# First batch: second-step loads all at once into other tiles' buffers, its evictions on two engines, the first MLP group ahead of other groups and weights

## The chip, the cores and the metric

The kernel runs on one core of one Trainium2 chip. The metric is the time on the device in microseconds (us), less is better. The engines that matter are PE (TensorE, matmuls), DVE (VectorE), ACT (ScalarE), POOL (GpSimd) and SP (SyncE, which here only issues DMAs). Each engine works through its own list of instructions in the order written at build time, and waits on semaphores for what other engines or DMAs must have finished first.

## The reference

The input x has 8 batches of 4224 rows of 192 elements, and weight_gen has 8 heads of 7 taps for each row. First a causal convolution whose taps are a softmax of weight_gen, then the Fourier mixing of FNet, a layer norm, and an MLP of 192 to 768 to 192 with ReLU:

```python
w = softmax(weight_gen)                        # over the 7 taps
x = einsum('bshk,bskhg->bshg', w, unfold(x))   # causal, 7 rows back
mixed = real(fft(fft(x, axis=1), axis=2))
u = x + mixed
un = (u - mean(u)) / sqrt(var(u) + 1e-6)       # over the 192 elements
out = u + maximum(un @ w_ch1, 0) @ w_ch2
```

## The kernel before

The 4224 rows of a batch are laid out as 128 partitions times 33, and are worked in 9 groups of 4 (the last has 1). A batch passes through these stages:

- conv: softmax of the taps (maximum and subtraction on DVE, lines 279 and 280, the exponential on ACT, line 282, then sum and reciprocal on DVE, lines 284 to 286), and the weighted sums u on DVE, POOL and PE. The first step of the Fourier transform follows for each group: matmul pg (line 471), two copies of ACT, and two DVE operations (lines 480 and 482) write a tile gt, which SP stores to a scratch tensor g_d in DRAM.
- transform: the second step. Its input is read back from g_d into six tiles g2 (line 507; the last with a second small load, line 509). Each tile has two halves e = 0 and 1: a group of matmuls into a PSUM bank pp (line 517), and evictions of pp into pq (lines 521 to 531): the rows in order, the mirrored rows (for e = 1 with a minus sign), and for the first two tiles a repeated part. That is 14 evictions for each half. There are two banks for pp, shared with eo.
- mix: for each group matmuls eo on pq (line 546), a copy ot of one half by ACT (line 551), and four DVE operations that add the result to u.
- norm: layer norm. For the first three groups of the first batch ("quick", groups 0 to 2) the statistics come from DVE (lines 580 and 581), for the others from ACT. ACT takes the root rs (line 582), DVE the reciprocal (line 593) and minus the mean times it (L596), and ACT writes un in four parts (line 601). For the quick groups un lies in two PSUM banks that are named like those of the MLP ("ph", three in number, taken in turn). Then un is split into two halves of 16 bits, hl: a cast on ACT (line 609) and two subtractions on DVE (lines 610 and 612; on POOL for later groups). A DMA transposes hl into ht (line 618).
- mlp: for each group six chunks ph (line 643), each five matmuls on ht and the halves of the first weight matrix, in a bank "ph"; ACT evicts each with ReLU to hh (line 649, or 653 with DVE's 654). The second matmuls po (line 666) run one group behind, and the result is added to u and stored.

The weights arrive as 64-bit numbers in words and are rebuilt by seven DVE operations for each piece (words_to_f32, lines 204 to 215). prep_w1 does this for the first matrix, with an ACT cast (line 220) and a DVE subtraction (line 221) for the halves w1h and w1l; eight copies by DMA (line 247) put the last rows in place. prep_w2 does it for the second matrix in three parts, w2_0, w2_1 and w2_2. Before the second step PE runs matmuls on values nobody needs (warm_pp, 20 of them; in the profile each shows as two records), and again before the first MLP group (warm_hl).

What sets the order. The stages are generators. The code adds them to a list of streams with a start and an end on a scale of groups (add), and run() draws them in turn; that is the order of priority. The build's scheduler then lays out each engine's list by this order and by its own simulated times. tc.issue_after(ins) keeps what stands inside from being laid out before ins; behind(ins, gen) does the same for each step of a generator, and queue(ins, ...) for a function. So the lists printed below are what the build made of it, and neither SP's nor any other engine's list changes at run time.

## Time and profile before

| | |
|---|---|
| median of 3 runs | 1138.15 us (1135.78 to 1138.86) |
| profiled execution: span from first to last instruction, the only time of it that the page gives | 1136.8 us |
| PE busy | 1082.2 us, 95% |
| DVE busy | 968.2 us, 85% |
| ACT busy | 814.5 us, 72% |
| POOL busy | 866.7 us, 76% |
| second step of batch 0 on PE (pp) | 82.28 to 95.60 us |
| first MLP chunk ph_0_0_0 begins | 115.05 us |
| second chunk ph_0_0_1 begins | 117.95 us |

In the rows of the timeline a time from the start stands first, then the duration of the whole row, the engine, the line, the operation, what it writes and reads, and how many instructions the row holds (x8). In square brackets stands how long the engine was idle before it and what ended that. In rows of stretches each engine's busy time comes with its number of instructions; the granted TensorE clock is 1.00 at full rate and 0.50 at half. In rows of waits the sum, the number and the longest are given.

### The profile page before, as it was taken

Reading aid. Unit: us, or ns where it says so; the run is one execution under the profiler, and the core shown is the slowest. Engines: PE = TensorE matmul, PEld = TensorE weight load, DVE = VectorE, ACT = ScalarE, POOL = GpSimd, SP = SyncE. Lnnn points to the kernel's source line nnn. Section 1 sums busy time; section 2 is a strip of 40 time slices with the busy share of each in tenths; the row PEclk is TensorE's granted clock in tenths of the full one; section 3 lists DMA queues with packets and bytes.
Section 4 is the critical chain, followed back from the end, with each engine's and each line's share of the span. In section 5 each row is a group of like instructions: output and inputs, shape, how many; then the busy total and the mean of one; then the engine's idle time right before and its main releaser. Section 6 shows DMA issues by size and latency. Waiting matters only on the chain.

```text
span 1136.8 us, 23769 instructions
## 1 busy us (share of the span) xinstructions
PE 1082.2 (95%) x8476; PEld 819.3 (72%) x8476; DVE 968.2 (85%) x1797; ACT 814.5 (72%) x2556; POOL 866.7 (76%) x747
## 2 busy tenths in 40 slices
PE   5986999999999999899999999999999999999998
PEld 3454677787777767677767877777768877787777
DVE  7988999879989999899988999999989996356443
ACT  4666785468975798568974799568965898589822
POOL 5979588699979999599969999699959999012200
PEclk9996999999999999999999999999999999999999
DMA  8353244614473248414562348414661234413221
GB/s 304 129 150 106 56 110 123 175 51 128 111 200 92 65 119 219 122 55 119 149 165 81 94 107 218 121 44 119 170 140 50 71 74 98 115 43 74 70 47 46
DMA packets 156504, 128.74 MB, mean 113 GB/s; under 512 B 108571, under 2 KB 133088, under 8 KB 156384
## 3 DMA queue, kind: packets, MB, share of 16 engines
q1 hardware_dynamic: 156384, 127.21, 42.2%
q8 instruction: 67, 1.10, 0.4%
q14 instruction: 53, 0.43, 0.1%
HBM read 61.46 MB, written 39.37 MB: 89 GB/s over the span
## 4 chain that ended last, share of the span: by engine, by line
PE 52%; DVE 16%; ACT 11%; issue 8%; POOL 7%; DMA 6%; SPq 1%; DVEq 0%; POOLq 0%; ACTq 0%
PE ph L643 22%; PE po L666 19%; DVE pr L441 6%; POOL u L450 6%; PE pp L517 4%; PE eo L546 3%; DMA g<-g_d 2%; ACT junk L590 2%; ACT junk L586 2%; PE pg L471 2%; PE pa L446 2%; ACT hh L653 2%; ACT un L601 2%; DVE hh L654 2%; DMA g_d<-gt 1%
## 5 line engine op out<-in xcount | busy, mean ns | idle before, releaser
L450 POOL TENSOR_TENSOR u<-u,pr 128x768 f32<-128x768 f32 (+1 forms) x390 | 644.5, 1675 | 71.0 <-DVE pr L441 49.6
L666 PEld LDWEIGHTS <-hh 128*128 128x128 f16 x4248 | 364.0, 98 | 74.1 <-DVE hh L654 2.2
L666 PE MATMUL po<-w2h,hh 128*128 128x192 f16 x2832 | 413.9, 246 | 1.2 <-DVE hh L654 1.0
L643 PE MATMUL ph<-ht,w1h 128*128 128x512 f16 (+1 forms) x1296 | 397.0, 363 | 5.4 <-DMA ht<-hl 2.5
L441 DVE TENSOR_TENSOR pr<-x_sb,wp 128x768 f32<-128x768 f32 (+1 forms) x415 | 354.5, 877 | 13.7 <-POOL u L450 9.9
L666 PE MATMUL po<-w2l,hh 128*128 128x192 f16 x1416 | 345.2, 246 | 0.0
L654 DVE SCALAR_TENSOR_TENSOR hh<-ph,hh 128x512 f16<-128x512 f32 (+1 forms) x390 | 246.4, 637 | 108.0 <-ACT hh L653 107.4
L653 ACT ACTIVATE hh<-ph 128x512 f16<-128x512 f32 (+1 forms) x390 | 213.3, 550 | 140.8 <-PE ph L643 114.6
L643 PE MATMUL ph<-ht,w1l 128*128 128x512 f16 (+1 forms) x864 | 311.2, 363 | 0.0
L643 PEld LDWEIGHTS <-w1h 128*128 128x128 f16 x1296 | 126.1, 99 | 93.2 <-issue 2.3
L601 ACT ACTIVATE un<-u,rs 128x192 f32<-128x192 f32 x264 | 123.7, 536 | 16.7 <-POOL hl L612 5.5
L643 PEld LDWEIGHTS <-w1l 128*128 128x128 f16 x864 | 85.4, 99 | 52.9 <-issue 5.3
L590 ACT ACTIVATE junk<-u,rs 128x192 f16<-128x192 f32 x252 | 114.2, 454 | 3.6
L610 POOL TENSOR_TENSOR hl<-un,hl 128x512 f16<-128x512 f32 (+1 forms) x69 | 75.2, 1090 | 51.9 <-issue 26.5
L586 ACT ACTIVATE junk<-u 128x192 f16<-128x192 f32 x252 | 90.8, 360 | 21.5 <-DVE u L556 17.9
L521 ACT COPY pq<-pp 97x204 f32<-97x204 f32 (+1 forms) x96 | 46.9, 489 | 57.4 <-PE pp L517 57.0
L546 PE MATMUL eo<-cs_sb,pq 97*128 97x97 f32 x544 | 84.2, 277 | 2.7 <-DVE u L556 2.7
L546 PEld LDWEIGHTS eo<-cs_sb,pq 97*128 97x128 f32 x544 | 78.1, 195 | 10.2 <-issue 4.7
L671 DVE SCALAR_TENSOR_TENSOR u<-po,isc,u 128x384 f32<-128x384 f32 (+1 forms) x122 | 72.8, 597 | 9.1 <-PE po L666 9.0
L464 POOL TENSOR_TENSOR sm<-u 128x382 f32<-128x382 f32 x64 | 65.3, 1021 | 5.8 <-DMA g_d<-gt 2.8
L599 POOL TENSOR_TENSOR rs<-rs 128x4 f32<-128x4 f32 (+1 forms) x63 | 12.8, 206 | 70.7 <-DVE rs L593 70.6
L666 PE MATMUL po<-w2f,hh 128*128 128x192 f32 x336 | 62.6, 328 | 0.0
(110 smaller groups left out, 1319.5 us busy)
## 6 DMA issues: line engine op xcount, KB each, us to landing
out_dram<-u SPq DMA_DIRECT2D x64, 384.0 KB
x_sb<-in_x_dram SPq DMA_DIRECT2D x48, 384.0 KB
g<-g_d SPq DMA_DIRECT2D x40, 336.0 KB
x_sb<-in_x_dram SPq DMA_DIRECT2D x8, 864.0 KB
g_d<-gt SPq DMA_DIRECT2D x32, 195.0 KB
g_d<-gt SPq DMA_DIRECT2D x32, 189.0 KB
w<-in_weight_gen_dram SPq DMA_DIRECT2D x6, 924.0 KB
x_sb<-in_x_dram SPq DMA_DIRECT2D x8, 672.0 KB
```

The lines of the kernel that those rows point to most:

```text
L441: last_product[b] = nc.vector.tensor_tensor(out=dst, in0=rows, in1=wk, op=ALU.mult)
L450: adder.tensor_tensor(out=u, in0=u, in1=pr, op=ALU.add)
L546: nc.tensor.matmul(eo[:, e, j, :], lhsT=pq[0:DH, e, r, r:r + P], rhs=cs_sb[:, e, :], start=True, stop=True)
L586: nc.scalar.activation(junk, uv[:, t, :], AF.Identity, accum_out=st[:, t, 0:1])
L590: nc.scalar.activation(junk, uv[:, t, :], AF.Square, bias=rs[:, 2, t:t + 1], accum_out=st[:, t, 1:2])
L601: nc.scalar.activation(halves[t // 2][:, t % 2, :], uv[:, t, :], AF.Identity, bias=rs[:, 1, t:t + 1], scale=rs[:, 0, t:t + 1])
L610: lo_eng.tensor_tensor(out=hl[:, t0:t1, 2 * P:3 * P], in0=src[:, 0:t1 - t0, 0:P], in1=hl[:, t0:t1, 0:P], op=ALU.subtract)
L643: last_ph[n] = nc.tensor.matmul(ph[:, 0:T], lhsT=wt[:, cs_], rhs=ht[:, 0:T, blk], start=(i == 0), stop=(i == len(terms) - 1))
L653: nc.scalar.activation(a[:, 0:T], ph[:, 0:T], AF.Relu)
L654: nc.vector.scalar_tensor_tensor(out=l[:, 0:T], in0=ph[:, 0:T], scalar=0.0, in1=a[:, 0:T], op0=ALU.max, op1=ALU.subtract)
L666: nc.tensor.matmul(po[t // 2][:, t % 2, :], lhsT=hx[:, t], rhs=wx[:, c2, :], start=(c2 == 0 and i == 0), stop=(c2 == NH - 1 and i == len(t ...
L671: nc.vector.scalar_tensor_tensor(out=lt, in0=po[t // 2][:, 0:t % 2 + 1], scalar=scales[0][:, 1:2] if f32 else isc, in1=lt, op0=ALU.mult, o ...
```

## The change

For the first batch alone:

- The six g2 tiles no longer take turns in three buffers. Three have the buffers of g2, two those of gt, and the last one of "fold" (a tile of conv). All their loads can be issued one after the other. The eight copies of w1h and w1l are kept behind the last g2 load.
- Of the evictions of pp the half e = 1 goes to DVE, 14 instructions; e = 0 stays on ACT.
- warm_pp has 32 matmuls, and reads f1_sb, a constant, so that it no longer waits for the last gt.
- A root of a constant is taken on ACT behind the last "up" copy of conv, which loads ACT's table for roots there.
- Group 0's un is written by DVE, in four operations that subtract the mean and multiply by rs; L596 falls away for this group.
- Group 2's mix is kept behind the root of group 0, and prep_w2 for parts 0 and 1 is queued after group 0's norm, no longer before its mix.

```diff
@@ -41,7 +41,8 @@
 F32_GROUPS = 7
 ACT_TAPS = {(0, 1): (0,), (0, 3): (0,), (0, 5): (0,1), (0, 7): (0,)}
 TURNS = {1: 'ddpdddd', 2: 'dpddpdd', 3: 'dpddpdp'}
-WARM = (20, 0, 12, 12)
+WARM = (32, 0, 12, 12)
+G2_FIRST = [("g2", TRI, 3)] * 3 + [("gt", TRI, 2)] * 2 + [("fold", 2, 3)]
 
 
 def row_table():
@@ -242,8 +243,8 @@
         w = words_to_f32(raws[0], None, "w1_1", ("ph", 3))
         split_f32(w, hi, lo, s1)
         for src, dst in ((hi, w1h1), (lo, w1l1)):
-            for i in range(2):
-                for j in range(2):
+            for i, j in ((0, 0), (0, 1), (1, 0), (1, 1)):
+                with tc.issue_after(last_g2[0].ins):
                     nc.sync.dma_start(dst[64 * j:64 * j + 64, i * PW:(i + 1) * PW], src[64 * i:64 * i + 64])
         for i in range(2):
             cs_ = slice(i * PW, (i + 1) * PW)
@@ -475,7 +476,7 @@
                 go = gt[:, at:at + J, :]
                 nc.scalar.copy(go[:, :, 0:DH:DH - 1], pg[:, 0:J, 0:DH:DH - 1])
                 up = sb.tile([P, 2, D - DH], F32, tag="up", name=f"up_{b}_{c}", bufs=2)
-                nc.scalar.copy(up[:, 0:J], pg[:, 0:J, DH:D])
+                last_up[b] = nc.scalar.copy(up[:, 0:J], pg[:, 0:J, DH:D])
                 fwd, rev = pg[:, 0:J, 1:DH - 1], up[:, 0:J, ::-1]
                 nc.vector.tensor_tensor(out=go[:, :, 1:DH - 1], in0=fwd, in1=rev, op=ALU.add)
                 last_tile[b] = gt
@@ -502,7 +503,8 @@
         for m0 in range(0, NM, TRI):
             nm = min(TRI, NM - m0)
             full = min(nm, NK1 // 3 - m0)
-            g2 = sb.tile([WL, TRI, D], F32, tag="g2", name=f"g2_{b}_{m0}", bufs=3)
+            home, rows, bufs = G2_FIRST[m0 // TRI] if b == 0 else ("g2", TRI, 3)
+            g2 = sb.tile([WL, rows, D], F32, tag=home, name=f"g2_{b}_{m0}", bufs=bufs)
             first = gv[m0 * W:m0 * W + 1, :]
             last_g2[b] = nc.sync.dma_start(g2[:, 0:full], bass.AP(first.tensor, first.offset, [[D, WL], [W * D, full], [1, D]]))
             if full < nm:
@@ -518,20 +520,24 @@
                                                   rhs=tab[0:kr, 0:w, :], start=True, stop=True)
                     yield (2 * m0 + e * nm + i + 1) / (2 * NM)
                 rows = pq[0:DH, e].rearrange("d r k -> d k r")
-                nc.scalar.copy(rows[:, k0:k0 + nk, :], pp[0:DH, 0:nk, 0:NT])
+                on_dve = b == 0 and e == 1
+                copy = nc.vector.tensor_copy if on_dve else nc.scalar.copy
+                copy(rows[:, k0:k0 + nk, :], pp[0:DH, 0:nk, 0:NT])
                 i0 = 1 if k0 == 0 else 0
                 i1 = nk - 1 if k0 + nk == NK1 else nk
                 dst, src = rows[:, P - k0 - i0:P - k0 - i1:-1, :], pp[0:DH, i0:i1, N2:NT - 1:-1]
                 if e == 0:
                     nc.scalar.copy(dst, src)
+                elif on_dve:
+                    nc.vector.tensor_scalar(out=dst, in0=src, scalar1=-1.0, scalar2=None, op0=ALU.mult)
                 else:
                     nc.scalar.mul(dst, src, -1.0)
                 n = min(KW - P - k0, nk)
                 if n > 0:
-                    nc.scalar.copy(rows[:, P + k0:P + k0 + n, :], pp[0:DH, 0:n, 0:NT])
+                    copy(rows[:, P + k0:P + k0 + n, :], pp[0:DH, 0:n, 0:NT])
 
     state, us, hls = {}, {}, {}
-    last_tile, last_pg, last_product, last_fold, last_gt, last_g2, last_pp = {}, {}, {}, {}, {}, {}, {}
+    last_tile, last_pg, last_product, last_fold, last_gt, last_up, last_g2, last_pp = {}, {}, {}, {}, {}, {}, {}, {}
     pending = {}
     total = B * NG
 
@@ -579,7 +585,7 @@
             for t in range(T):
                 nc.vector.bn_stats(out=bn[:, t, :], in_=uv[:, t, :])
                 last_bn[b, g] = nc.vector.bn_aggr(out=st[:, t, :], in_=bn[:, t, :])
-            nc.scalar.activation(rs[:, 0, 0:T], st[:, 0:T, 1], AF.Sqrt, bias=eps_t)
+            last_sqrt[b, g] = nc.scalar.activation(rs[:, 0, 0:T], st[:, 0:T, 1], AF.Sqrt, bias=eps_t)
             neg = -1.0
         else:
             for t in range(T):
@@ -591,13 +597,20 @@
                                      accum_out=st[:, t, 1:2])
             nc.scalar.activation(rs[:, 0, 0:T], st[:, 0:T, 1], AF.Sqrt, bias=eps_t, scale=1.0 / D)
         nc.vector.reciprocal(out=rs[:, 0, 0:T], in_=rs[:, 0, 0:T])
-        if quick or b == 0:
+        first = NG * b + g == 0
+        if first:
+            pass
+        elif quick or b == 0:
             for t in range(T):
                 nc.vector.tensor_scalar(out=rs[:, 1, t:t + 1], in0=st[:, t, 0:1], scalar1=rs[:, 0, t:t + 1],
                                         scalar2=neg, op0=ALU.mult, op1=ALU.mult)
         else:
             nc.gpsimd.tensor_tensor(out=rs[:, 1, 0:T], in0=rs[:, 2, 0:T], in1=rs[:, 0, 0:T], op=ALU.mult)
         for t in range(T):
+            if first:
+                nc.vector.tensor_scalar(out=halves[t // 2][:, t % 2, :], in0=uv[:, t, :], scalar1=st[:, t, 0:1],
+                                        scalar2=rs[:, 0, t:t + 1], op0=ALU.subtract, op1=ALU.mult)
+                continue
             nc.scalar.activation(halves[t // 2][:, t % 2, :], uv[:, t, :], AF.Identity,
                                  bias=rs[:, 1, t:t + 1], scale=rs[:, 0, t:t + 1])
         yield 0.5
@@ -706,7 +719,7 @@
     def next_conv(b):
         yield from behind(last_product[b - 1].ins, conv(b))
 
-    last_word, last_split, last_lo, last_bn, last_ph, scales = [], [], {}, {}, {}, []
+    last_word, last_split, last_lo, last_bn, last_sqrt, last_ph, scales = [], [], {}, {}, {}, {}, []
     add(0.0, 1.0, conv(0))
     run(0.5)
     loaded = load_weights()
@@ -716,8 +729,11 @@
             for f, arg in calls:
                 f(arg)
 
+    root = cpool.tile([P, 1], F32, name="root")
+    with tc.issue_after(last_up[0].ins):
+        nc.scalar.activation(root, eps_t, AF.Sqrt)
     with tc.issue_after(last_pg[0].ins):
-        WARM[0] and keep_warm(("po", 2), "pp", ident32, last_tile[0][:, 3, 0:P], WARM[0])
+        WARM[0] and keep_warm(("po", 2), "pp", ident32, f1_sb[:, 0], WARM[0])
     add(0.0, 1.0, transform(0))
     run()
     lp = last_product[0].ins
@@ -727,13 +743,16 @@
             break
     tap8, tap9 = ((lambda n: tap_step(1, n), n) for n in (8, 9))
     queue(lp, (prep_w1, loaded[0]))
-    for i in range(2):
-        queue(last_split[-1].ins, (prep_w2, i))
+    split1 = last_split[-1].ins
     for g in range(QUICK):
-        add(0.0, 1.0, behind(last_split[-1].ins, mix(0, g)))
+        gen = behind(split1, mix(0, g))
+        add(0.0, 1.0, behind(last_sqrt[0, 0].ins, gen) if g == 2 else gen)
         run()
         add(0.0, 1.0, norm(0, g))
         run()
+        if g == 0:
+            for i in range(2):
+                queue(split1, (prep_w2, i))
     for g, call in ((0, tap8), (1, (prep_w2, 2)), (1, tap9)):
         queue(last_lo[g].ins, call)
 
```

Line numbers of the changed kernel are 1 to 13 higher than those before: L280 there is L279 here, L588 is L582, L614 is L601, L622 and L623 are L609 and L610, L662 is L649.

On SP, in the second step of batch 0, stood before:

```order
44 L507 DMA g2_0_0_714<-g_d0_89 112x4x192
45 L507 DMA g2_0_4_732<-g_d0_89 112x4x192
46 L507 DMA g2_0_8_750<-g_d0_89 112x4x192
47 L247 DMA w1h1_83<-w1h_1_892 64x384 x4
48 L247 DMA w1l1_84<-w1l_1_893 64x384 x4
49 L507 DMA g2_0_12_766<-g_d0_89 112x4x192
50 L507 DMA g2_0_16_782<-g_d0_89 112x4x192
51 L507 DMA g2_0_20_798<-g_d0_89 112x192
52 L509 DMA g2_0_20_798<-g_d0_89 68x192
```

and now stands:

```order
44 L509 DMA g2_0_0_728<-g_d0_89 112x4x192
45 L509 DMA g2_0_4_746<-g_d0_89 112x4x192
46 L509 DMA g2_0_8_764<-g_d0_89 112x4x192
47 L509 DMA g2_0_12_780<-g_d0_89 112x4x192
48 L509 DMA g2_0_16_796<-g_d0_89 112x4x192
49 L509 DMA g2_0_20_812<-g_d0_89 112x192
50 L511 DMA g2_0_20_812<-g_d0_89 68x192
51 L248 DMA w1h1_83<-w1h_1_906 64x384 x4
52 L248 DMA w1l1_84<-w1l_1_907 64x384 x4
```

The three later tiles' loads moved ahead of the eight copies.

On ACT, from the casts of group 1 (hl_0_1) to the eviction of the first MLP chunk (hh_0_0_0); w_1 is the taps of batch 1, whose exponential L282 this is. Before:

```order
97 L609 CAST hl_0_1_1050<-un_0_1_0_1029 128x2x192
98 L609 CAST hl_0_1_1050<-un_0_1_1_1030 128x2x192
99 L282 ACT_TABLE_LOAD
100 L282 ACTIVATE w_1_812<-w_1_812 128x1344
101 L601 ACTIVATE un_0_2_0_1073<-u_0_2_220,rs_0_2_1071 128x192
102 L601 ACTIVATE un_0_2_1_1074<-u_0_2_220,rs_0_2_1071 128x192
103 L601 ACTIVATE un_0_2_0_1073<-u_0_2_220,rs_0_2_1071 128x192
104 L601 ACTIVATE un_0_2_1_1074<-u_0_2_220,rs_0_2_1071 128x192
105 L609 CAST hl_0_2_1094<-un_0_2_0_1073 128x2x192
106 L649 ACTIVATE hh_0_0_0_1126<-ph_0_0_0_1120 128x512
107 L609 CAST hl_0_2_1094<-un_0_2_1_1074 128x2x192
108 L649 ACTIVATE hh_0_0_1_1137<-ph_0_0_1_1128 128x512
```

and now:

```order
80 L622 CAST hl_0_1_1060<-un_0_1_1_1040 128x2x192
81 L283 ACT_TABLE_LOAD
82 L283 ACTIVATE w_1_826<-w_1_826 128x1344
83 L588 ACT_TABLE_LOAD
84 L588 ACTIVATE rs_0_2_1081<-st_0_2_1080,eps_t_79 128x4
85 L614 ACTIVATE un_0_2_0_1083<-u_0_2_220,rs_0_2_1081 128x192
86 L614 ACTIVATE un_0_2_1_1084<-u_0_2_220,rs_0_2_1081 128x192
87 L614 ACTIVATE un_0_2_0_1083<-u_0_2_220,rs_0_2_1081 128x192
88 L614 ACTIVATE un_0_2_1_1084<-u_0_2_220,rs_0_2_1081 128x192
89 L622 CAST hl_0_2_1104<-un_0_2_0_1083 128x2x192
90 L622 CAST hl_0_2_1104<-un_0_2_1_1084 128x2x192
91 L662 ACTIVATE hh_0_0_0_1136<-ph_0_0_0_1130 128x512
```

The root rs_0_2, which stood eight rows ahead of the exponential before (row 92, behind the casts of hl_0_0), now stands behind the exponential with a table load of its own, and the eviction hh_0_0_0 moved behind both casts of hl_0_2. un_0_2_0 and un_0_2_1 lie in banks "ph", of which ph_0_0_1 takes the first.

On DVE, the last rows ahead of the subtraction L280 (now L281), whose result the exponential takes. Before:

```order
178 L593 RECIPROCAL rs_0_1_1027<-rs_0_1_1027 128x4
179 L580 BN_STATS bn_0_2_1075<-u_0_2_220 128x6 x4
180 L596 TENSOR_SCALAR rs_0_1_1027<-st_0_1_1026,rs_0_1_1027 128x1 x4
181 L581 BN_AGGR st_0_2_1070<-bn_0_2_1075 128x2 x4
182 L610 TENSOR_TENSOR hl_0_0_993<-un_0_0_0_972,hl_0_0_993 128x2x128
183 L612 TENSOR_TENSOR hl_0_0_993<-un_0_0_0_972,hl_0_0_993 128x2x64
184 L610 TENSOR_TENSOR hl_0_0_993<-un_0_0_1_973,hl_0_0_993 128x2x128
185 L612 TENSOR_TENSOR hl_0_0_993<-un_0_0_1_973,hl_0_0_993 128x2x64
186 L279 TENSOR_REDUCE wp_1_811<-w_1_812 128x192
187 L593 RECIPROCAL rs_0_2_1071<-rs_0_2_1071 128x4
188 L280 TENSOR_TENSOR w_1_812<-w_1_812,wp_1_811 128x1344
189 L596 TENSOR_SCALAR rs_0_2_1071<-st_0_2_1070,rs_0_2_1071 128x1 x4
```

and now:

```order
194 L561 TENSOR_TENSOR u_0_2_220<-u_0_2_220,eo_0_2_1069 128x4x97
195 L562 TENSOR_TENSOR u_0_2_220<-u_0_2_220,eo_0_2_1069 128x4x95
196 L605 TENSOR_SCALAR rs_0_1_1037<-st_0_1_1036,rs_0_1_1037 128x1 x4
197 L214 SCALAR_TENSOR_TENSOR t_w2_1_1017<-raw_w4_418,pa_w2_1_1015 128x384
198 L623 TENSOR_TENSOR hl_0_0_983<-un_0_0_0_966,hl_0_0_983 128x2x128
199 L625 TENSOR_TENSOR hl_0_0_983<-un_0_0_0_966,hl_0_0_983 128x2x64
200 L623 TENSOR_TENSOR hl_0_0_983<-un_0_0_1_967,hl_0_0_983 128x2x128
201 L625 TENSOR_TENSOR hl_0_0_983<-un_0_0_1_967,hl_0_0_983 128x2x64
202 L280 TENSOR_REDUCE wp_1_825<-w_1_826 128x192
203 L586 BN_STATS bn_0_2_1085<-u_0_2_220 128x6 x4
204 L216 TENSOR_TENSOR w2f_87<-pw_w2_1_1016,t_w2_1_1017 128x384
205 L281 TENSOR_TENSOR w_1_826<-w_1_826,wp_1_825 128x1344
```

The statistics and the reciprocal of group 2 now stand behind the last hl of group 0 or behind L281, and operations on w2_1 stand where there were none. Between the first L552 (now L558) and this subtraction stand five operations on w2_0 and w2_1 before, ten now.

## The prediction

> **What bounds the kernel now.** I read the page first, then busy time by stretches with the clock granted, then PE's row of the waits, and last the timelines of PE, DVE, ACT and SP between 72 and 130 us.
>
> ```profile
> span 1136.8 us, 23769 instructions
> PE 1082.2 (95%) x8476; PEld 819.3 (72%) x8476; DVE 968.2 (85%) x1797; ACT 814.5 (72%) x2556; POOL 866.7 (76%) x747
> 97.00:120.00 23.00, 10.24 (x40) 5.99 (x39) 22.61 (x76) 13.75 (x28) 22.84 (x16) 0.58 0.27 50
> 120.00:150.00 30.00, 30.00 (x170) 22.15 (x169) 28.08 (x55) 22.50 (x67) 15.31 (x13) 0.98 0.21 45
> 300.00:1100.00 800.00, 787.19 (x6663) 600.50 (x6662) 683.77 (x1238) 610.17 (x1892) 620.87 (x550) 1.00 0.43 110
> PE pp L517 <- DMA g<-g_d: 10.3, 6, 2.9
> ```
>
> The stretches give start and end, length, then busy us (and instructions) of PE, PEld, DVE, ACT, POOL, the granted clock, the DMA share and GB/s. From 120 us on PE is full (30.00 of 30, later 787 of 800) and works through a fixed list, so a shift of the first MLP group is a shift of the end. In 97 to 120 it is DVE that is full (22.61 of 23): the first group waits there for DVE and ACT. The last row, of PE's waits after 120 us, holds the largest idle time left for a late PE to lose itself in: 10.3 us in six pieces, the longest 2.9.
>
> ```profile
> 74.75 4.70 PE L494 MATMUL warm_pp<-gt,ident 128*128 128x128 f32 x40 [1.22 <-DVE gt L482]
> 82.28 0.91 PE L517 MATMUL pp<-te_sb,g 102*97 102x102 f32 x8 [2.83 <-DMA g<-g_d]
> 84.51 1.68 PE L517 MATMUL pp<-te_sb,g 102*97 102x102 f32 x8 [0.51 <-ACT pq L531]
> 90.09 1.06 PE L517 MATMUL pp<-te_sb,g 102*97 102x102 f32 x8
> 92.11 0.94 PE L517 MATMUL pp<-te_sb,g 102*97 102x102 f32 x8
> 94.01 0.56 PE L517 MATMUL pp<-te_sb,g 102*97 102x102 f32 x4
> 95.04 0.56 PE L517 MATMUL pp<-to_sb,g 102*97 102x102 f32 x4 [0.47 <-ACT pq L528]
> 115.92 0.38 PE L643 MATMUL ph<-ht,w1l 128*128 128x512 f16 x1
> 117.95 0.58 PE L643 MATMUL ph<-ht,w1h 128*128 128x512 f16 x1 [1.65 <-ACT hh L649]
> 76.84:80.25 3.41, 2.62 (x24) 1.00 0.28 78
> 80.25:83.66 3.41, 1.38 (x16) 1.00 1.10 267
> 83.66:87.07 3.41, 2.90 (x18) 0.50 0.58 124
> 117.79:121.20 3.41, 3.25 (x11) 0.50 0.11 21
> 121.20:124.61 3.41, 3.41 (x19) 1.00 0.00 0
> ```
>
> The last five rows are PE alone by stretches; the clock stands behind the busy time. Two PE waits lie on the path: for the first g2 tile (2.83 us), and, behind chunk ph_0_0_0 of the first MLP group, for ACT's hh_0_0_0 (to 117.95).
>
> **The loads, at nothing.**
>
> ```profile
> 78.46 1.39 SPq L507 DMA_DIRECT2D g<-g_d  x3
> 85.54 5.10 SPq L507 DMA_DIRECT2D g<-g_d  x3
> ```
>
> The loads that move were issued from 85.54 on, behind the w1 copies. Still no pp matmul waits for one: among the pp rows only the first has a DMA as releaser. The cover is pp itself, at half clock from 83.66. Issued early they should land before 90, so also a faster pp isn't held. The eight w1 copies go behind them, landing some 7 us later, far ahead of ph at 115. The x loads of batch 1 come about 4.5 us earlier; nothing that PE waits for before 150 us needs them. If pp outran the loads, each of three tiles could cost up to the 1.4 us between issues.
>
> **Warming and the clock, a gain of about 2.1 us.** 32 matmuls make 64 records; at 4.70/40 = 0.1175 us each they last 7.5 us. Without the wait for gt (1.22) they begin at about 73.5 and end at 81, leaving 1.3 us before pp in place of 2.83. The stretch 80.25 to 83.66, busy for 1.38, was followed by half clock; it would now be busy for about 2.2. The stretch before it, busy for 2.62, was followed by full clock. So the bound lies between 1.38 and 2.62; 2.2 is nearer the upper end, and where the stretches fall in a run isn't fixed: I take the clock as kept (6 in 10). Then two tiles that took 90.09 - 84.51 = 5.58 us cold take about 1.9 each as at 92.11 to 94.01, a gain of 1.8, and most of the 0.47 before 95.04 goes: 2.1 in all, so pp ends at 93.5. Bounds: 0 with the clock lost, 2.4 with no wait on evictions.
>
> [...]
>
> **Evictions on DVE, at nothing, up to 0.5.** Fourteen of ACT's evictions go to DVE.
>
> ```profile
> 84.61 0.53 ACT L528 ACTIVATE pq<-pp 97x187 f32<-97x187 f32 x1
> 71.92 0.35 DVE L480 TENSOR_TENSOR gt<-pg,up 128x190 f32<-128x190 f32 x1
> 90.23 0.62 DVE L221 SCALAR_TENSOR_TENSOR w1l<-pw_w,sc_w,w1h 128x384 f16<-128x384 f32 x1 [3.24 <-ACT w1h L220]
> 97.20 0.37 DVE L552 TENSOR_TENSOR eo<-eo,ot 128x194 f32<-128x194 f32 x1 [1.18 <-ACT ot L551]
> ```
>
> The trace has no strided eviction on DVE. Bounds: 0.35 (190 elements read from PSUM there) and 0.53 (the same copy on ACT), so 4.9 to 7.4 us; I take 0.35. DVE idles 3.24 before 90.23 and 1.18 before 97.20, 4.4 that cover most; the rest pushes weight work (w2) behind the first group's start, counted next. PE at full clock is held by neither engine for more than a few tenths, since 92.11 to 94.01 shows a tile at 1.9 with ACT doing both halves. DVE reaches group 0 two evictions and two w2 steps behind pp's end, 93.5 + 0.7 + 0.9 = 95.1: just when ot comes, 1.6 us behind pp's end as before (95.60 to 97.20).
>
> **Group 0 on DVE: 2.4 us longer.**
>
> ```profile
> 97.48 0.55 DVE L207 TENSOR_SCALAR pa_w<-raw_w 128x384 int32<-128x384 int32 x1
> 106.73 0.57 DVE L596 TENSOR_SCALAR rs<-st,rs 128x1 f32<-128x1 f32 x4
> 108.80 0.37 DVE L581 BATCH_NORM_AGGREGATE st<-bn 128x2 f32<-128x6 f32 x4
> 110.11 0.28 DVE L612 TENSOR_TENSOR hl<-un,hl 128x128 f16<-128x128 f32 x1
> 111.89 1.55 DVE L280 TENSOR_TENSOR w<-w,wp 128x1344 f32<-128x1344 f32 x1
> 115.36 1.55 DVE L284 TENSOR_REDUCE wp<-w 128x192 f32<-128x1344 f32 x1
> 119.24 1.36 DVE L286 RECIPROCAL wp<-wp 128x192 f32<-128x192 f32 x1
> 102.65 1.28 ACT L582 ACT_TABLE_LOAD   x1
> 109.47 0.30 ACT L582 ACTIVATE rs<-st,eps_t 128x4 f32<-128x4 f32 x1
> 113.96 1.32 ACT L282 ACTIVATE w<-w 128x1344 f32<-128x1344 f32 x1
> 115.19 1.81 ACT L601 ACTIVATE un<-u,rs 128x192 f32<-128x192 f32 x4
> 116.95 0.46 ACT L609 CAST hl<-un 128x384 f16<-128x384 f32 x1
> ```
>
> Between the first L552 and the subtraction L280 (w_1, batch 1's taps; lines here are those of before) stood 5 steps of w2; by the order there are now 10: 5 x 0.46 = 2.3 (0.46 is start to start, 97.48 to 97.94). The four un on DVE come in at 0.28 each, as L612 (bounds 0.26 to 0.55), 1.1. Out go L596 x4 of group 0 (0.48), the aggregates of group 2 (0.37) and one reciprocal (0.13): 1.0. Net +2.4, so L280 ends at 113.44 - 2.1 + 2.4 = 113.7. Up to the last hl of group 0 the same count gives 4 w2 steps more and group 2's four statistics fewer, +1.1 - 2.1: its transpose goes about 1 us earlier. The table load at 102.65 moves ahead of pp, under PE's and DVE's work; with DVE full behind it (22.61 of 23), that brings no more than this 1 us.
>
> **What ph_0_0_1 now waits for: 3.3 us later.** Before, rs_0_2's root ran at 109.47, ahead of the exponential; un_0_2 followed the exponential at once, and hh_0_0_0 came behind its first cast. Now ACT has, in this order, exponential, table load, rs_0_2's root, un_0_2 x4, both casts, hh_0_0_0. The exponential runs 113.75 to 115.05; the load (1.28) and root (0.30) end at 116.65. DVE meanwhile holds the reduction L284 (1.5, from 115.6 to 117.1), then the reciprocal, one w2 step, L285 and the first L596, 0.13 + 0.46 + 0.27 + 0.1: un_0_2 starts at 118.05 in place of 115.19. It takes 1.8, the casts 0.4 each: 120.65. DVE, with the other L596 (0.35), two w2 steps (0.92) and the reciprocal L286 (1.36) behind that, also gets to hl_0_2 at 120.7 and leaves the bank at 121.25. ph_0_0_1 needs un_0_2's bank, so it starts at about 121.3 and not at 117.95: **+3.3**. Bounds: +2.4 with quick un and evictions, +4.5 with both at their dear ends. That ph_0_0_0 itself comes 1 us earlier is worth nothing then: it ends at 115 and its successor is late.
>
> PE idles for 6 us there, 1.65 before. The clock was half in 117.79 to 121.20, with 3.25 us of work, some 1.6 lost; with stretches placed as before the same amount is lost in the next one, elsewhere up to 1.7 more. I take 0.5.
>
> **Sum:** 3.3 + 0.5 = 3.8 on a span of 1136.8: 1140.6. The profiled span stands 1.35 under the median of the runs, 1138.15, so the time is 1138.15 + 3.8 = **1142.0**.
>
> **Rivals.**
> *Cold* (17%): the warming doesn't hold the clock, pp ends as before, and all of group 0 comes 2.1 us later: 1138.15 + 5.9 = 1144.0, to 1146.5 with dear evictions. For it: the 1.3 us that are still idle, and evictions that alternate with weight work on DVE. Against: 64 records in place of 40.
> *Given back* (20%): the delay is lost in a later idle time of PE, at most the longest wait for g2, 2.9: 1138.15 + 3.8 - 2.9 = 1139.1. For it: x loads 4.5 us earlier; against: pg, ahead of each of these waits, is on PE too and shifts with it.
> *Faster* (15%): DVE sets the pace of the exponential and runs ahead by the whole gain: 2.1 of pp and 1.2 of the table load. Then L280 ends at 110.1, the exponential at 111.5, load and root at 113.1, un_0_2 starts by 114.2, casts end by 116.7: ph_0_0_1 at 116.8, 1.1 earlier, and 1.6 of half clock less: 1138.15 - 2.7 = 1135.5. It decides if L280 ends before about 110.3, which needs the w2 steps not to lie in group 0; the order speaks against it, the full DVE of before makes each step taken out worth its time.
> Early loads bringing nothing is in all four.
>
> **How the numbers follow.** 40% for the sum, 1140 to 1144 by its bounds; the rivals as given; 8% for gains that I can't name. The range reaches to the faster case below and the cold one above: 1134.5 to 1146. A measurement here can tell 0.3% (3.4 us) from no change, so slower begins at 1141.6 and faster at 1134.7: slower is three quarters of the sum's case and all of the cold one, 0.47; faster two thirds of its own case, whose row-by-row gain could as well be 3 to 4, and the unnamed gains, 0.18; the same takes the rest, 0.35.
>
> **What would show it.** Right: PE's second group of ph rows starts at 120 to 122 behind a wait of 5 us or more on DVE hl or ACT hh; ACT shows a table load between the exponential and rs_0_2's root; pp ends by 94 at clock 1.0; no pp but the first waits for a DMA. Wrong: ph_0_0_1 before 118, or half clock in pp, or a busy PE in 300 to 1100 us that has won 2 us or more on its 787 of 800.

## The result: 0.45% slower, and the profile after

| | before | changed |
|---|---|---|
| median of 20 runs | 1137.57 us (1133.34 to 1139.60) | 1141.70 us (1136.31 to 1147.47) |
| ratio to before, 95% interval | | 1.0045 (1.0034 to 1.0057) |
| span of the profiled execution | 1136.8 us | 1140.9 us |

The forecast was 1142.0 us, between 1134.5 and 1146.0, with 0.47 for slower. The time is 0.3 us from it. The path to it is another one, as the traces and runs below show: in the profiled execution the first MLP group came 7 us late and not 3.8, and about 3 us of that were given back later.

The page of the changed kernel, its first two lines:

```profile
span 1140.9 us, 23808 instructions
PE 1083.4 (95%) x8500; PEld 822.2 (72%) x8500; DVE 972.0 (85%) x1811; ACT 812.3 (71%) x2539; POOL 867.6 (76%) x747
```

PE's timeline from the warming matmuls to the second chunk of the first MLP group (changed kernel):

```profile
73.43 7.31 PE L495 MATMUL warm_pp<-f_sb,ident 128*128 128x128 f32 x64
83.61 1.09 PE L519 MATMUL pp<-te_sb,g 102*97 102x102 f32 x8 [2.87 <-DMA g<-g_d]
...
86.00 1.68 PE L519 MATMUL pp<-te_sb,g 102*97 102x102 f32 x8
...
96.26 0.56 PE L519 MATMUL pp<-to_sb,g 102*97 102x102 f32 x4 [0.51 <-ACT pq L530]
96.66 2.26 PE L552 MATMUL eo<-cs_sb,pq 97*128 97x97 f32 x16
...
118.67 0.61 PE L656 MATMUL ph<-ht,w1h 128*128 128x512 f16 x1 [1.66 <-ACT w L283]
...
120.35 0.63 PE L656 MATMUL ph<-ht,w1l 128*128 128x512 f16 x1
124.62 0.58 PE L656 MATMUL ph<-ht,w1h 128*128 128x512 f16 x1 [3.63 <-DVE hl L625]
```

The warming ends at 80.7 as reckoned, but the first g2 tile landed at 83.6 instead of 82.2, so PE was idle for 2.87 us all the same. A tile of pp takes over 1.5 us for each half, as before (the row at 86.00 has 1.68 us for 8 matmuls): the granted clock was 0.50 from 84.20 to 91.03. Group 0's first eo follows at 96.66, where before it stood at 95.44:

```profile
95.44 2.51 PE L546 MATMUL eo<-cs_sb,pq 97*128 97x97 f32 x16
```

ph_0_0_1 starts behind a wait on DVE's hl of group 2, at 124.62 in place of 117.95.

The later landing comes from the store of gt ahead of the load. Both kernels issue the last of it at the same time (75.02 before, 75.08 changed), but SP then waits 2.9 us for it before (first row) and 4.2 in the changed kernel (second):

```profile
SPq L507 <- DMA g_d<-gt: 2.9, 1, 2.9
```

```profile
SPq L509 <- DMA g_d<-gt: 4.2, 1, 4.2
```

Why the store took 1.3 us longer in this execution stays open.

ACT in the same kernel, from the table load for the exponential to hh_0_0_0:

```profile
115.14 1.28 ACT L283 ACT_TABLE_LOAD   x1
117.32 1.32 ACT L283 ACTIVATE w<-w 128x1344 f32<-128x1344 f32 x1 [0.90 <-DVE w L281]
118.66 1.28 ACT L588 ACT_TABLE_LOAD   x1
119.96 0.30 ACT L588 ACTIVATE rs<-st,eps_t 128x4 f32<-128x4 f32 x1
121.56 1.82 ACT L614 ACTIVATE un<-u,rs 128x192 f32<-128x192 f32 x4 [1.31 <-DVE rs L605]
123.33 0.84 ACT L622 CAST hl<-un 128x384 f16<-128x384 f32 x2
124.06 0.59 ACT L662 ACTIVATE hh<-ph 128x512 f32<-128x512 f32 x1
```

This is the chain of the prediction, link for link. DVE's timeline in the changed kernel, from the first evictions to the last hl that ph_0_0_1 waits for:

```profile
86.09 0.50 DVE L525 COPY pq<-pp 97x204 f32<-97x204 f32 x1 [3.88 <-PE pp L519]
86.45 0.47 DVE L532 TENSOR_SCALAR pq<-pp 97x187 f32<-97x187 f32 x1
...
98.42 0.37 DVE L558 TENSOR_TENSOR eo<-eo,ot 128x194 f32<-128x194 f32 x1
...
107.53 0.86 DVE L611 TENSOR_SCALAR un<-u,st,rs 128x192 f32<-128x192 f32 x2
...
115.73 1.56 DVE L281 TENSOR_TENSOR w<-w,wp 128x1344 f32<-128x1344 f32 x1
...
118.97 1.57 DVE L285 TENSOR_REDUCE wp<-w 128x192 f32<-128x1344 f32 x1
...
122.16 1.38 DVE L287 RECIPROCAL wp<-wp 128x192 f32<-128x192 f32 x1
...
124.17 0.30 DVE L625 TENSOR_TENSOR hl<-un,hl 128x128 f16<-128x128 f32 x1
```

A strided eviction on DVE takes 0.36 from start to start (86.09 to 86.45), at the low end of the bounds. From L558 to the end of L281 it is 98.42 to 117.29, 18.9 us, where before L552 to the end of L280 took 16.2: the forecast was 2.4 more, it is 2.6.

Of the changed kernel, PE alone in three stretches that overlap (the second ends at 84.20, where the clock falls), then all engines by stretches, then PE's waits behind 120 us:

```profile
80.20:83.60 3.40, 0.54 (x5) 1.00 0.80 197
80.79:84.20 3.41, 0.59 (x7) 1.00 0.99 237
83.60:87.00 3.40, 3.40 (x22) 0.59 1.12 235
```

```profile
120.00:150.00 30.00, 26.37 (x138) 18.34 (x137) 29.96 (x57) 16.82 (x50) 15.21 (x12) 0.86 0.17 33
300.00:1100.00 800.00, 787.82 (x6681) 602.82 (x6680) 683.88 (x1240) 617.38 (x1910) 619.96 (x551) 1.00 0.43 110
```

```profile
PE pp L519 <- DMA g<-g_d: 10.9, 7, 3.6
PE ph L656 <- DVE hl L625: 3.6, 1, 3.6
```

In the first three rows PE goes on at half clock after 0.59 us of work in the 3.41 up to the fall. The waits for g2 tiles are not smaller than before (10.9 against 10.3 us): the late PE has not lost itself in them.

How late PE is, as the start of the ph matmul with the same number in both traces (counted through the whole run, us):

```
ph matmul    before   changed  later by
     1       115.05    118.67     3.62
     6       117.95    124.62     6.67
    16       122.51    129.52     7.01
   121       176.56    183.55     6.99
   211       229.99    233.26     3.27
   301       282.40    292.50    10.09
   601       422.11    426.92     4.81
  1001       617.55    622.06     4.51
  2160      1131.19   1135.26     4.07
```

Up to 180 us the 7 us stay. Then the difference swings between 3 and 10 and ends at 4.1. Part of that is order alone, since the lists themselves differ: read from the traces, at least 1438 of PE's 8412 matmul records (the warming ones left out) stand elsewhere in the changed kernel, and PE's order is that of before again only from 963 us on, in batch 6 (the batches are 0 to 7). The build lays every list out by simulated times, and here a changed head changed them all. The prediction went by the lists around the first group only. A swing by itself is no proof of it: with only the warming changed, whose lists are those of before from 106 us on, the same difference goes from -1.1 to -4.2 and back to -2.5 us.

### The profile page after: what moved, and what is told of

It reads as the page before. It is cut to its first block, busy times and chain, and to the rows that moved or that the text cites. A ratio compares the mean times of both kernels' runs of the same rounds, so it can differ in the third digit from the quotient of the medians.

```text
span 1140.9 us, 23808 instructions
## 1 busy us (share of the span) xinstructions
PE 1083.4 (95%) x8500; PEld 822.2 (72%) x8500; DVE 972.0 (85%) x1811; ACT 812.3 (71%) x2539; POOL 867.6 (76%) x747
## 4 chain that ended last, share of the span: by engine, by line
PE 52%; DMA 3%; POOL 2%; DVE 1%; issue 1%; ACT 1%; SPq 0%; DVEq 0%; POOLq 0%
PE ph L656 22%; PE po L679 21%; PE pp L519 3%; PE eo L552 3%; PE pg L472 2%; DMA g<-g_d 1%; DMA g_d<-gt 1%; POOL u L451 1%; POOL hl L623 0%; DVE pr L442 0%; DVE hh L667 0%; POOL hl L625 0%; DVE wp L285 0%; ACT un L614 0%; ACT w L283 0%
## 5 line engine op out<-in xcount | busy, mean ns | idle before, releaser
L614 ACT ACTIVATE un<-u,rs 128x192 f32<-128x192 f32 x260 | 121.6, 535 | 20.5 <-DVE rs L605 8.0
L623 POOL TENSOR_TENSOR hl<-un,hl 128x512 f16<-128x512 f32 (+1 forms) x69 | 75.8, 1099 | 56.6 <-issue 26.5
L596 ACT ACTIVATE junk<-u,rs 128x192 f16<-128x192 f32 x252 | 114.3, 454 | 4.1
L552 PE MATMUL eo<-cs_sb,pq 97*128 97x97 f32 x544 | 86.9, 276 | 4.2 <-DVE u L562 4.2
L552 PEld LDWEIGHTS eo<-cs_sb,pq 97*128 97x128 f32 x544 | 79.9, 195 | 10.7 <-issue 4.8
L525 ACT COPY pq<-pp 97x204 f32<-97x204 f32 (+1 forms) x90 | 43.8, 487 | 55.9 <-PE pp L519 55.0
```

Source lines behind the costliest of these rows:

```text
L552: nc.tensor.matmul(eo[:, e, j, :], lhsT=pq[0:DH, e, r, r:r + P], rhs=cs_sb[:, e, :], start=True, stop=True)
L596: nc.scalar.activation(junk, uv[:, t, :], AF.Square, bias=rs[:, 2, t:t + 1], accum_out=st[:, t, 1:2])
L614: nc.scalar.activation(halves[t // 2][:, t % 2, :], uv[:, t, :], AF.Identity, bias=rs[:, 1, t:t + 1], scale=rs[:, 0, t:t + 1])
L623: lo_eng.tensor_tensor(out=hl[:, t0:t1, 2 * P:3 * P], in0=src[:, 0:t1 - t0, 0:P], in1=hl[:, t0:t1, 0:P], op=ALU.subtract)
```

## The experiments

All twelve are kernels of which only the part named is edited. Each ratio is to the kernel before, run on the same chip alongside; it need not be the quotient of two medians (late_old_lists has 1141.87 against 1136.53, a quotient of 1.0047, and a ratio of 1.0030). "Head" below is the delay of the 16th ph matmul in the profiled execution against before, where the first group is done with its waits; "end" is that of the last.

Head and end go by one execution of each kernel. In nearly all runs here the span stands 1.8 us under the run's time, so the profile of before is an execution of about 1138.6 us by estimate, while before's medians alongside were 1135.31 (the first four experiments), 1136.53 (the next four) and 1137.77 (the last four). Counted from those medians each end would be 1 to 3 us larger. And some profiles are of the quickest execution of their kernel (exp_late, w2_late, loads alone) or of the slowest (un_only, late_old_lists).

Some kernels are said below, and in the expectations, to have the lists of before behind the head. In the traces the orders of PE, DVE, ACT and POOL agree with before throughout (loads alone), from 106 us on (warming alone), from 182 (changed_no_un, the change without un on DVE and without the wait) and from 208 (evictions alone, and late_old_lists, with 72 warming matmuls); between the head and there some rows of these three stand elsewhere. Those of the run with 40 warming matmuls agree with the changed kernel's from 116 us on.

**The three theories** were these. A: group 2's root and its table load behind the exponential make ph_0_0_1 late. B: DVE's extra work makes it late. C or L: what happens at 120 us doesn't decide, but the lists behind it that are laid out anew. H stands against L: a shift of the head is a shift of the end.

### Group 2's mix set free

```diff
-        add(0.0, 1.0, behind(last_sqrt[0, 0].ins, gen) if g == 2 else gen)
+        add(0.0, 1.0, gen)
```

> The changed kernel without the wait that holds group 2's mix behind group 0's root; all else as changed. By the order, rs_0_2's root then stands ahead of the exponential of w_1 again (behind the casts of hl_0_0), and un_0_2 follows the exponential without a table load; DVE still has ten w2 steps ahead of L281. Theory A (the root and its table load behind the exponential are what makes ph_0_0_1 late): un_0_2 starts right behind the exponential, about 2.7 us sooner, ph_0_0_1 at about 121.5 us instead of 124.6, and the time falls by about 3 us, to 1138.5. Theory B (DVE's extra work, evictions and w2 steps, makes it late): ph_0_0_1 stays at 124 or later and the time at 1141.5. Theory C (what happens at 120 us is not what decides; the lists behind it are laid out differently): ph_0_0_1 is earlier but the time does not follow.

Measured: 1145.01 us, ratio 1.0079 (1.0059 to 1.0099). ACT's timeline in this kernel, from group 2's root to hh_0_0_0:

```profile
110.27 0.30 ACT L588 ACTIVATE rs<-st,eps_t 128x4 f32<-128x4 f32 x1 [1.28 <-DVE st L587]
...
113.09 1.28 ACT L283 ACT_TABLE_LOAD   x1
114.38 1.32 ACT L283 ACTIVATE w<-w 128x1344 f32<-128x1344 f32 x1
115.61 1.81 ACT L614 ACTIVATE un<-u,rs 128x192 f32<-128x192 f32 x4
...
118.15 0.60 ACT L662 ACTIVATE hh<-ph 128x512 f32<-128x512 f32 x1
```

PE's row for ph_0_0_1, and DVE's for the subtraction ahead of the exponential:

```profile
118.80 0.58 PE L656 MATMUL ph<-ht,w1h 128*128 128x512 f16 x1 [0.69 <-ACT hh L662]
```

```profile
112.66 1.53 DVE L281 TENSOR_TENSOR w<-w,wp 128x1344 f32<-128x1344 f32 x1
```

un_0_2 now follows the exponential at once, and ph_0_0_1 starts 4.6 us behind the end of L281 (118.80 less 114.19), as before the change (4.5); in the changed kernel it was 7.3. So the order on ACT is worth 2.7 us at ph_0_0_1: theory A holds there. In this execution the first tile also landed at 81.75 and the clock stayed full through pp (0.94 us for 8 matmuls, against the 1.68 above), which together brought eo 3.4 us forward. The head is 1.4 us late instead of 7.0. Yet the ratio is 1.0079 where the changed kernel has 1.0045, some 4 us more: theory C. The end of this profile is 6.0 us late, 4.6 of them lost behind the head.

### Evictions back on ACT

```diff
-                on_dve = b == 0 and e == 1
+                on_dve = False
```

> The changed kernel with the evictions of the half e = 1 of the first batch back on ACT; all else as changed. Theory A: the order on ACT around the exponential is unchanged, so ph_0_0_1 stays late; DVE has 8 w2 steps in place of 10 ahead of L281, 0.9 us: ph_0_0_1 at about 123.5, time 1140.7. Theory B: DVE's evictions (14, some 4.5 us) are the cause: ph_0_0_1 back to 119 to 120, time 1137 to 1138.

Measured: 1137.81 us, ratio 1.0020 (1.0003 to 1.0037). Going by the time alone this would be theory B. The trace says otherwise: ph_0_0_1 starts at 123.79, as theory A had it, and the head is 6.9 us late, as in the changed kernel. The end of this profile is 0.4 us early: 7.3 us are won behind the head. A time that agrees with an expectation is no proof of its reason.

### The exponential kept behind group 2

```diff
-    for g, call in ((0, tap8), (1, (prep_w2, 2)), (1, tap9)):
+    for g, call in ((1, (prep_w2, 2)), (2, tap8), (2, tap9)):
```

> The changed kernel with the exponential step of w_1 (batch 1's taps: maximum, subtraction, exponential) kept behind group 2's last hl instead of group 0's. ACT then has no table load between the groups' roots and un. Theory A: un_0_2 no longer waits for the exponential at all; ph_0_0_0 is followed by ph_0_0_1 at once, at about 118.5 in this trace's scale, 6 us sooner; the taps of batch 1 come about 8 us later. If these are not due, the time falls by 6 us, to 1136. Theory C: batch 1's conv starts later on POOL and DVE, and its second step pp_1 gives the 6 us back or more: time 1141 or above.

Measured: 1146.86 us, ratio 1.0094 (1.0074 to 1.0113). ph_0_0_1 starts at 116.64, 8 us sooner than in the changed kernel, of which pp, with a full clock (11.5 us from its first matmul to the first eo, 13.05 in the changed kernel) and the first tile 1.3 us sooner, brought 2.9; the head is 2.9 us early. The end is 4.6 us late: theory C. Whether batch 1's late taps or the new lists cost it, this run can't tell.

### The second matrix behind group 1

```diff
-        if g == 0:
-            for i in range(2):
-                queue(split1, (prep_w2, i))
-    for g, call in ((0, tap8), (1, (prep_w2, 2)), (1, tap9)):
+    for g, call in ((0, tap8), (1, (prep_w2, 0)), (1, (prep_w2, 1)), (1, (prep_w2, 2)), (1, tap9)):
```

> The changed kernel with the rebuilding of the second matrix (w2_0, w2_1) kept behind group 1's last hl, so that none of its steps lies in DVE's work for group 0: 0 in place of 10 steps of 0.46 us ahead of L281. ACT's order (exponential, table load, root of group 2) as changed. Theory A and B both: L281 ends 4.6 us sooner, so does the exponential, and un_0_2 starts 3 to 4.6 us sooner: ph_0_0_1 at about 120.5. But w2's 21 steps (9.7 us) then come behind group 1 and in among what follows the exponential (root's reciprocal, hl of group 2): where they hold up hl_0_2, ph_0_0_1 stays at 124. Time 1138 if the first, 1142 to 1145 if the second.

Measured: 1164.33 us, ratio 1.0253 (1.0232 to 1.0275), far outside both cases. ph_0_0_0 started only at 121.05 and ph_0_0_1 at 123.14, and behind the head a further 20 us were lost. This kernel says nothing of the w2 steps alone.

### Only un on DVE

The kernel before with the part of the change in norm that writes group 0's un on DVE:

```diff
+            if first:
+                nc.vector.tensor_scalar(out=halves[t // 2][:, t % 2, :], in0=uv[:, t, :], scalar1=st[:, t, 0:1],
+                                        scalar2=rs[:, 0, t:t + 1], op0=ALU.subtract, op1=ALU.mult)
+                continue
```

> The kernel before with one part of the change: group 0's un written by DVE instead of ACT. At the head this adds some 1.1 us to DVE's work and takes 2.3 from ACT's; ph_0_0_1 should move by less than 1 us. But with this one part the build lays out 3161 of 13888 PE instructions, 900 of 1799 of DVE and 221 of 752 of POOL in another order, up to batch 6. Theory H (the head sets the end: a shift of the first MLP group goes through): time within 1 us of before. Theory L (the lists behind the head were laid out anew, and that is what costs): ph_0_0_1 within 1 us of before, but the time 4 to 7 us above.

Measured: 1146.49 us, ratio 1.0076 (1.0053 to 1.0098). Head 0.4 us early, end 12.2 us late in the profile. This profile is of the slowest of the ten executions (1150.80 us), so its 12.2 is more than the kernel's. Four instructions moved from ACT to DVE cost as much as the whole change or more, above the 4 to 7 us of theory L, and in this trace all of it behind 300 us: theory L. One place can be read. The second step of batch 2, in this kernel (first row) and before (second), and PE alone in the stretch behind it, in the same order:

```profile
347.04 1.65 PE L517 MATMUL pp<-te_sb,g 102*97 102x102 f32 x8 [2.34 <-DMA g<-g_d]
```

```profile
346.88 0.91 PE L517 MATMUL pp<-te_sb,g 102*97 102x102 f32 x8 [0.65 <-ACT hh L653]
```

```profile
346.70:353.50 6.80, 6.46 (x31) 0.50 0.47 120
```

```profile
346.70:353.50 6.80, 6.62 (x62) 1.00 0.73 205
```

Before, the g2 tiles are there when PE comes; now PE waits 2.34 us for the first, goes on at half clock, and does 31 matmuls in 6.8 us in which it did 62. That is 2.34 - 0.65 + 3.4 = 5.1 us at one place.

### The change without un on DVE and without the wait

The edit of "Group 2's mix set free", and `first = False`; all other parts stay.

> The changed kernel without two of its parts (group 0's un on DVE, and the wait of group 2's mix on group 0's root): loads, evictions on DVE, 32 warming matmuls and the early table load stay. Its lists behind the head are those of before, row for row: 42 of PE's 13888 instructions stand elsewhere, none behind the first twentieth. Theory L: no cost but the head's own; ph_0_0_1 about 1 to 2 us later than before, the time -1 to +2. Theory H as I had it says the same of the sum only if ph_0_0_1 is that near to before; if ph_0_0_1 is 3 us late and the time is 3 us late too, H holds.

Measured: 1141.87 us, ratio 1.0039 (1.0020 to 1.0059). In the profile the head is 0.7 and the end 2.4 us late, in an execution of 1141.02. By the ratio the kernel is 4.4 us above before; the expectation was -1 to +2, and neither theory gives so much with the head and the lists so near to before. About 2 of the 4.4 don't show in the profile's 2.4, as the profile of before is of an execution above its median. Of the 1.8 us that are lost behind the head in the profile, PE's idle time is 1.7. The loads, the evictions and the warming alone, below, bring 0.7, 0.8 and -1.0 parts in a thousand, none clear of none. The root taken early and the later place of w2's parts 0 and 1 are in this kernel too, and no run has either of them alone. So why a kernel with nearly the old lists is as slow as the changed one stays open.

### A late head with old lists, and one with new

```diff
-WARM = (20, 0, 12, 12)
+WARM = (72, 0, 12, 12)
```

> The kernel before with 72 warming matmuls in place of 20: PE reaches the second step at about 91.7 us, 9.4 later, at full clock, so that the end of pp and all of the head come some 7 to 8 us later than before. The lists behind the head stay as before (66 PE instructions moved, all in the first twentieth). It measures how much of a late head reaches the end. Theory H: all of it, +7 us. Theory with slack: the idle time of PE behind 126 us (17.8 us in before) takes part of it: +2 to +5.

The second kernel has the same and, in keep_warm's call, `f1_sb[:, 0]` for `last_tile[0][:, 3, 0:P]`:

> As the run with 72 warming matmuls, but they read f1_sb and do not wait for gt, so they start and end 1.3 us sooner: the head is 1.3 us less late. With this the build lays out the lists behind the head anew (3926 of PE's 13888 instructions stand elsewhere, 1081 of DVE's 1799). Theory H: 1.3 us faster than the run whose lists are as before. Theory L: slower than it, by 2 us or more.

Measured: 1141.87 us, ratio 1.0030 (1.0012 to 1.0047) with old lists, and 1145.66 us, 1.0062 (1.0039 to 1.0084) with new. In the profiles the first has its head 3.9 us late (eo was 7.0 late; 3 us of that go in the waits up to ph, ahead of where the slack was looked for) and its end 4.5; at 230 us, where its lists are those of before, it is 3.7 late: what is late there goes through to the end within 1 us, theory H. The second has its head 1.2 us late, 2.7 less than the first, and its end 6.4: theory L, as different lists add 5.2 us behind the head. The intervals of the two ratios overlap, but the runs, made alongside, don't: the slowest of the twelve with old lists took 1144.13 us, the quickest of the six with new lists 1144.74. This pair is the one that shows theory L without leaning on a profile.

### 40 warming matmuls

```diff
-WARM = (32, 0, 12, 12)
+WARM = (40, 0, 12, 12)
```

> The changed kernel with 40 warming matmuls in place of 32: 80 records of 0.1175 us, 73.4 to 82.8 us, up to where the first g2 tile lands. The lists behind the head stay those of the changed kernel (8 PE instructions moved, all at the head); on DVE 6 w2 steps lie ahead of L281 in place of 10, 1.8 us less. If the clock is a term as the prediction had it: it stays full through pp, the first eo begins at 93.5 to 94.5 in place of 96.7, ph_0_0_1 by 120 to 121 in place of 124.6, and the time falls by 3 to 4 us to 1138 (ratio to before 1.001). If the clock falls all the same, only the w2 steps count: 1.8 us, ratio 1.003.

Measured: 1139.18 us, ratio 1.0012 (0.9995 to 1.0028). PE's timeline in this kernel, from the warming to ph_0_0_1:

```profile
74.12 9.10 PE L495 MATMUL warm_pp<-f_sb,ident 128*128 128x128 f32 x80
83.14 0.91 PE L519 MATMUL pp<-te_sb,g 102*97 102x102 f32 x8
...
91.20 0.94 PE L519 MATMUL pp<-te_sb,g 102*97 102x102 f32 x8
...
94.19 0.56 PE L519 MATMUL pp<-to_sb,g 102*97 102x102 f32 x4 [0.51 <-ACT pq L530]
...
121.27 0.58 PE L656 MATMUL ph<-ht,w1h 128*128 128x512 f16 x1 [3.63 <-DVE hl L625]
```

PE has no idle time before pp and keeps its clock (0.91 and 0.94 us for 8 matmuls in these rows, 1.68 at half clock): pp ends 2.1 us sooner than in the changed kernel, of which 0.5 is the first tile's earlier landing. ph_0_0_1 is 3.35 us sooner, with four w2 steps fewer ahead of L281 as well, and the end 2.8. These are the lists of the changed kernel behind the head, so this pair shows a shift going through. The ratio goes from 1.0045 to 1.0012: with the lists kept, most of what the change costs goes with these few microseconds at the head.

### Each of three parts alone

Warming alone is `WARM = (36, 0, 12, 12)` on `f1_sb[:, 0]` in the kernel before; loads and evictions alone are those parts of the change's diff.

> The kernel before with 36 warming matmuls on f1_sb in place of 20 on gt, 73.4 to 81.9 us, and nothing else; the lists behind the head are those of before (36 PE instructions moved, all at the head). With the clock kept through pp the first eo begins 1.5 to 2.2 us sooner; if a shift of the head goes through to the end, the time is 1 to 2 us under before. If the eo gain is lost to DVE's list ahead of the exponential, no change.

> The kernel before with the change's loads alone: six tiles in the buffers of g2, gt and fold, loaded one after the other, the w1 copies behind them. Only SP's list differs (8 of 402 rows). The prediction put this at nothing: ratio 1.000, within 0.002. If PE was held by the later loads in some runs, or the w1 copies now come too late for ph, it shows as -0.002 or +0.003.

> The kernel before with the change's evictions alone: the half e = 1 of the first batch on DVE. The lists behind the head are those of before but for 8 of DVE's rows (14 PE instructions moved). The changed kernel showed 0.36 us between starts for a strided eviction on DVE, 14 of them 4.4 us. The prediction put it at 0 to 0.5 us; one w2 step more lies ahead of L280. Ratio 1.000 to 1.002; ph_0_0_1 0 to 1 us later than before. If DVE's list is what holds the head, 1.003 or more.

| alone | median | ratio to before | head | end |
|---|---|---|---|---|
| warming, 36 | 1137.04 | 0.9990 (0.9977 to 1.0004) | -1.7 | -2.5 |
| loads | 1138.41 | 1.0007 (0.9993 to 1.0021) | -1.5 | -2.7 |
| evictions | 1139.13 | 1.0008 (0.9995 to 1.0020) | +1.0 | -0.5 |

None differs from before by more than these runs can tell. The loads' profile is an execution of 1135.91, the quickest of its twelve, so its -2.7 isn't the kernel's. The root taken early, the later place of w2 and group 2's wait were not run alone.

### What is lost behind the head, in all of them

Two things can be read from each trace behind the head: PE's idle time between matmuls (before 17.8 us behind 126) and the time at half clock, of which half is lost where PE works (31 matmuls in 6.8 us in place of 62, above; before 10.2 us, in three pieces of 3.4 at 223.6, 397.7 and 599.1). The pieces are counted whole, so what PE idles inside one is counted twice. "Sum" is the head's delay plus the change in idle time plus half the change in time at half clock:

```
                  head   idle  half clock/2   sum    end
changed           +7.0   -0.1     -1.7       +5.2   +4.1
g2_free           +1.4   +3.7      0.0       +5.1   +6.0
act_evict         +6.9   -3.2     -3.4       +0.3   -0.4
exp_late          -2.9   +7.0      0.0       +4.1   +4.6
w2_late           +3.9  +12.6    +10.2      +26.7  +23.7
un_only           -0.4   +5.2     +8.5      +13.3  +12.2
changed_no_un     +0.7   +1.7      0.0       +2.4   +2.4
late_old_lists    +3.9   -0.4     +1.7       +5.2   +4.5
late_new_lists    +1.2   +2.0     +3.4       +6.6   +6.4
changed_warm40    +4.0   -0.6      0.0       +3.4   +1.2
warm_only         -1.7   -0.5      0.0       -2.2   -2.5
loads_only        -1.5   -1.1      0.0       -2.6   -2.7
evict_only        +1.0   +0.2     -1.7       -0.5   -0.5
```

For nine of the thirteen the sum is within 1 us of the end. For the changed kernel and for un_only 1.1 us remain, for the one with 40 warming matmuls 2.2 and for w2_late 3, which I didn't locate. Each row is one execution, and the pieces at half clock differ from run to run (the mean clock of the changed kernel's 20 runs goes from 0.976 to 0.986), so a row explains its trace and no median.

A rival remains for the medians. The 20 runs of the changed kernel stood at half clock for 42 us in the mean, before's runs alongside the experiments for 32 to 34 (for the 20 runs of before no clock is on record). By the slope of 0.44 us for each us in the last section that is 3.6 to 4.4 us, as much as the whole difference; this is an estimate. Part of that time is idle time of PE at the head, where half clock costs nothing (in before the clock was 0.50 from 104.13 to 107.54, without a matmul), so it is not shown that the clock alone makes the change slower, nor that it doesn't.

## Why the prediction was right, and where it wasn't

- **Loads at nothing:** held. No pp matmul but the first waits for a DMA, and alone they give 1.0007 (0.9993 to 1.0021). The loads of x for batch 1 did not come 4.5 us earlier: SP issues them from 91.15 us on, before from 91.06.
- **Warming keeps the clock, 2.1 us gained:** this step failed in the profiled execution, in which the clock was half from 84.2 to 91.0 and eo came 1.2 us late. The chance was about so: of six profiles with 32 warming matmuls three kept the clock through pp (eo 1.6 to 2.6 us sooner than before) and three lost it (eo 0.7 to 1.3 us later). The size was a little less: from the start of the first pp matmul to that of the first eo it is 13.2 us before, and 11.5 in the three that kept the clock and with 40 matmuls, a gain of 1.7. What failed in the changed kernel's profile is the landing taken as fixed at 82.2: it was 83.6. But the landing alone doesn't decide. PE was idle ahead of pp for 1.37, 1.47 and 1.90 us in the three that kept the clock, and for 1.65, 2.39 and 2.87 in those that lost it. Nor does a bound between 1.38 and 2.62 us of work in a stretch, as the prediction took it: the trace of before itself has a fall behind 2.90 us of work, and a full clock behind 1.53 (last section). The place of the stretches, which the prediction took as not fixed, differs between these two traces: the clock fell in pp at 83.66 before and at 84.20 in the changed kernel, 0.54 us apart on a scale of 3.41. With 40 matmuls, which left no idle time ahead of pp, the clock stayed in the one profile. The rival "cold" named the loss.
- **Evictions at nothing:** held: 0.36 us apiece, alone 1.0008 (0.9995 to 1.0020).
- **Group 0 on DVE 2.4 us longer:** held, 2.6. Each un took 0.38 and not 0.28, from 0.86 for two with their overlap.
- **ph_0_0_1 behind the exponential, a table load, the root and L287:** held. From the end of L281 to ph_0_0_1 the walk made 7.6 us, it was 7.3, and 4.6 with group 2's mix set free. The whole step came out as 6.7 and not 3.3 at ph_0_0_1, since the 2.1 of the clock were missing and the first tile landed 1.3 later. The 0.5 for the half clock behind it came out as 0.3 (7.0 at the 16th matmul).
- **A shift of the first group is a shift of the end:** this step failed too, and with it the path to the sum. It holds, within 2 us, where the lists behind the head are the same (late_old_lists +3.9 to +4.5, and 40 against 32 warming matmuls -3.0 to -2.8; but changed_no_un +0.7 to +2.4). The changed kernel's lists aren't those of before, up to batch 6. In its profile 2.9 of 7.0 us were given back, of which 1.7 are one piece at half clock less; that it is the lists which gave the rest back is likely by late_new_lists and un_only, where they cost time, but no run shows it for this kernel. The rival "given back" had the sign and the size by chance, for a reason that didn't occur: the waits for g2 are as long as before.
- **Its own signs:** ACT's table load stood where it said, and no pp but the first waited for a DMA. The others failed: ph_0_0_1 came at 124.6 and not at 120 to 122, behind a wait of 3.6 us and not 5 or more, as ph_0_0_0 was late too; pp ended behind 96 and not by 94. Half clock in pp was one of its signs of being wrong.
- **The sum, 1142.0:** it met the median by luck, by two errors against each other, 3.2 us too little at the head and 2.9 too much behind it.

## What to carry to other kernels

Where a scheduler lays out every list by simulated times, compare the lists to their end before pricing an edit at its own place: four moved instructions cost 0.76% here, none of it where they stand. To measure one step apart, look for a variant whose later lists come out unchanged, and read how late the same instruction is at several points of both traces, not only the time. And reckon work put in to keep a clock up against the spread of the landings of what comes next, not the one in the profile at hand: 32 warming matmuls, reckoned against a landing at 82.2, kept the clock in three profiles of six, with landings up to 83.65; 40, which left no idle time, kept it in the one profile there is.
